# Decoding 64-bit weights without the folding pass, with the range check on a second load, in a linear-attention and expert kernel

## The chip, the cores and the metric

The kernel runs on one core of a Trainium2 chip. The metric is the device time of one execution in microseconds (us), the median over several runs. A profiled execution gives the trace; it covers the span from the first to the last instruction, and its own device time lies a little above the span. The engines are called PE (TensorE: matmuls; PEld is its weight load), DVE (VectorE), ACT (ScalarE), POOL (GpSimd) and SP (SyncE, which here only issues DMAs).

## What is computed

Two stages. The first is a linear attention with a decay for each key element, over 4 batches, 8 heads, 768 steps and heads of 48; the second is a gated expert layer on the 3072 tokens that come out, of width 384 with 1536 inner columns.

```python
# attention: state is 48 x 48 for each batch and head
for t in range(S):
    state = alpha[:, :, t, :, None] * state + einsum('bhd,bhe->bhde', k[:, :, t], v[:, :, t])
    y[:, :, t] = einsum('bhd,bhde->bhe', q[:, :, t], state)
# expert layer: x is y as 3072 x 384
xn = x / sqrt(mean(x * x, axis=-1, keepdims=True) + 1e-06) * rms_g
g, val = xn @ w_gate, xn @ w_val                       # 384 x 1536 each
out = (g * (1 / (1 + exp(-g))) * val) @ w_out          # 1536 x 384
```

q, k, v, alpha and rms_g are fp32. The three weights come as 64-bit floats, and the kernel sees each as one 64-bit integer, that is as two 32-bit words: `lo` (the last 32 bits of the fraction) and `hi` (sign, 11 bits of exponent, 20 of fraction).

## The kernel before

**Precision.** Every operand of a matmul is split in two f16 numbers, a high part (the value cast to f16, mostly by ACT) and a low part (what is left, mostly by DVE), and each product is three matmuls: high by high, high by low, low by high (`SPLIT`).

**Chunks and groups.** The tokens are cut in 24 chunks of 128 (6 for each batch, the batches in turn), and the chunks in seven groups, `GROUPS = [4, 2, 2, 4, 4, 4, 4]`. For a chunk, `attention` does on DVE two scans (L643) with a reciprocal between, the products of q and k with the decays (L661, L666) and the low parts (L673, L691, L700); on ACT the high parts (L477, in the helper `split_hi`, which also sums what it writes into a column of `stat`); on PE the scores (L741, L750), the output y (L821, L831) and the update of the state (L849). The masked scores (L756) are cast by ACT (L808); their low part is taken by DVE (L811) or, for the chunks in `LOW_A`, by a matmul with a negative identity (L792) and ACT (L802). Then come the RMS norm (L873 on ACT, L879 and L893 on DVE, a power on POOL), x in two parts (L897 on ACT, L900 on DVE) and its transpose by DMA into xT (L911, on SP's queue).

**Expert layer.** For a group and each of 12 steps of 128 inner columns, `expert_in` does two halves of nine matmuls (L1029), gate and value, each into one of three `mm` buffers in PSUM; ACT takes the silu of the gate (L1040), DVE multiplies by the value (L1046), ACT casts the high part of h (L477) and DVE takes the low part (L1059). Group 0's first `EARLY = 5` steps are done twice, for two chunks each. After its 12 steps a group's output is summed by `expert_out`: 36 matmuls for each chunk (L1099) into `mm_po`, which is one of the same three `mm` buffers, evacuated by DVE into `ob` (L1113) and stored (L1117). Group 0's four chunks are done as three and one (`SIDE`).

**Weights.** `decode` turns a tile of 128 x 768 64-bit words into f16 high and low parts, for 12 input tiles i0 to i11 (w_gate and w_val, 786 KB by two DMAs, L504) and 6 output tiles o0 to o5 (w_out, one DMA). Two `raw` and two `wu` buffers hold the tiles in work. The steps for one tile are:

- the fold, ACT (L514): |hi| times 2^-111 as an fp32, written to the compact words `u`; it brings the exponent in range, drops the sign, and its accumulated sum goes to `wsum` for a range check
- the tail, DVE (L523): `lo` shifted right by 29
- the sign: for 11 tiles (`SIGN_A`) ACT writes an f16 zero of the right sign into the top half of each `lo` word (L532, an f16 at every 8 bytes); for the others DVE puts it there with the sign bit of `hi` (L526)
- the join, DVE (L537): `u` shifted left by 3, or `lo`, which is the fp32 word
- the high part, ACT (L477, with its sum in `stat`), and the low part, DVE (L545). For the tiles of `LOW_W`, i0 and i6, the join goes to two `y` buffers in PSUM (L556), and the low part is made by a matmul with a negative identity (L566, after PE has claimed the buffers at L550) and ACT (L572).

At the end `verdict` compares the sums in `stat`, `ssq`, `wsum` and `dec` with bounds; if one is outside, a branch runs `general`, a slow version for any input.

**The order of the work.** Nothing above is issued in the order of the code. Each step is an operation with an engine, a cost and the buffers that it uses, and `Plan.order` sorts all of them once, with a due time for each that comes from the tables at the top (`PACE`, `GAP`, `FIRST_DUE`, `AHEAD`, `STRIDE`, `LATE`, `NUDGE`, `HOLD`). The outcome is one fixed queue of instructions for each engine, DMA issues on SP among them; an engine runs its queue strictly in order and waits at the head for what is not done yet.

Of the kernel before, what the change touches and what calls it, by code (L numbers as in the profile page):

```python
# [81 lines left out]
LATE = dict(
    abs=-6.0, al=-47.4, claim=73.0, gd=-9.8, h=-40.7, hl=79.1, join=-68.1, join2=22.9,
    k16=-35.5, kl=33.1, load=7.2, mask=-8.5, neg=-6.2, ob=-61.3, po=138.5, q16=57.8, ql=37.3,
    rec=-14.7, rest=-50.9, sc=-9.9, scan=23.1, sd=12.9, sign=39.5, sl=-13.0, sq=-22.1, ss=-57.2,
    st=0.5, u=-55.5, v16=6.0, vl=-2.7, wh=9.4, wh2=34.9, wl=-23.8, wneg=-1.0, x=-3.2, x16=-27.9,
    xl=-107.4, y=-20.0, zero=-6.0,
)
# [240 lines left out]
def tile_attn_moe(  # L329
# [134 lines left out]
    o_x = o_h + NH  # L464
    o_kk = o_x + len(LOW_W)
# [28 lines left out]
    def decode(src, dst, name, col):  # L494
# [4 lines left out]
        def load():  # L499
# [9 lines left out]
            t["top"] = raw.bitcast(F16).rearrange("p (n four) -> p n four", four=4)[:, :, 1]  # L509
            t["hif"] = raw.bitcast(F32).rearrange("p (n two) -> p n two", two=2)[:, :, 1]  # L510

        def fold():
# [1 line left out]
            nc.scalar.activation(  # L514
                t["u"].bitcast(F32),
                t["hif"],
                AF.Abs,
                scale=W_FOLD,
                accum_out=wsum[:, col - o_w : col - o_w + 1],
            )  # L520

        def tail_bits():
            nc.vector.tensor_scalar(t["lo"], t["lo"], 29, None, op0=ALU.logical_shift_right)  # L523

        def sign():
            nc.vector.scalar_tensor_tensor(  # L526
                t["lo"], t["hi"], -(2**31), t["lo"], op0=ALU.bitwise_and, op1=ALU.bitwise_or
            )

        def sign_zero():  # L530

            nc.scalar.activation(t["top"], t["hif"], AF.Copy, scale=W_NONE)  # L532

        half = [slice(n * (NW // 2), (n + 1) * (NW // 2)) for n in range(2)]

        def join():
            nc.vector.scalar_tensor_tensor(  # L537
                t["u"], t["u"], 3, t["lo"], op0=ALU.logical_shift_left, op1=ALU.bitwise_or
            )
# [4 lines left out]
        def low():
            nc.vector.tensor_tensor(dst[:, 1], t["u"].bitcast(F32), dst[:, 0], op=ALU.subtract)  # L545
# [9 lines left out]
        def join_at(n):  # L555
            nc.vector.scalar_tensor_tensor(  # L556
                t["ps"][n].bitcast(I32)[:, : NW // 2], t["u"][:, half[n]], 3, t["lo"][:, half[n]],
                op0=ALU.logical_shift_left, op1=ALU.bitwise_or,
            )
# [16 lines left out]
        oa = add("ACT", "abs", fold, [o], [raw, wu])  # L576
        ot = add("DVE", "rest", tail_bits, [o], [raw], lock=True)
        if name in SIGN_A:
            os = add("ACT", "zero", sign_zero, [ot], [raw])
# [766 lines left out]
```

## Time and profile before

| | before |
|---|---|
| median of 3 runs | 536.62 us (536.5 to 537.01) |
| the profiled execution | 537.63 us, of which 535.4 are the span |
| granted TensorE clock, mean | 0.997 |
| PE busy | 498.2 us (93%), 4808 matmuls |
| DVE busy | 397.4 us (74%), 743 instructions |
| ACT busy | 269.0 us (50%), 695 instructions |
| POOL busy | 22.5 us (4%) |
| DMA | 50.51 MB, mean 94 GB/s |

The page of the profile has the span in 40 slices of 13.4 us, with the busy share of each engine in tenths. A line for a group of instructions gives the line of the code, the engine, the operation with what it writes and reads, the count, the busy time, the mean of one in ns, and the idle time just before it with what ended most of that. In the table of stretches each engine has its busy time and count, and behind them stand the granted clock, the busy share of the DMA engines and GB/s. In a list of waits stand the sum in us, the count and the longest. In the chain and the timeline stand the start and the length in us.

### The profile page before, as it was taken

What the parts mean: (1) busy time and instruction counts of PE and PEld (TensorE: products, weight loads), DVE (VectorE), ACT (ScalarE), POOL (GpSimd) and SP (SyncE); (2) the same over time, 40 slices, a digit from 0 to 9 for tenths busy, and PEclk for the clock granted to TensorE, in tenths of its full rate; (3) what the DMA queues carried; (4) which work ended last, traced back from release to release, by engine and by line L of the source; (5) the groups of instructions that cost most, each with busy time, mean ns of one, the idle gap of its engine ahead of it and who ended that gap; (6) DMA issues with size and microseconds to landing.
All of it is one profiled execution on the core that took longest, in us unless ns stands there. A gap on an engine that the chain in (4) does not pass through costs nothing.

```text
span 535.4 us, 11809 instructions
## 1 busy us (share of the span) xinstructions
PE 498.2 (93%) x4808; PEld 298.9 (56%) x4808; DVE 397.4 (74%) x743; ACT 269.0 (50%) x695; POOL 22.5 (4%) x55
## 2 busy tenths in 40 slices
PE   1548699899999999999999999999999999999996
PEld 1437464466886887544566544556545555544453
DVE  6998889999999999995799956899767541133331
ACT  3889989854655565433554434645256420133300
POOL 3001000001000100000000000000000000000000
PEclk9999989999999999999999999999999999999999
DMA  8997747553543631951034820412100001000001
GB/s 193 254 256 211 211 150 227 189 151 98 141 99 91 126 86 27 202 117 53 1 84 115 185 75 1 99 36 61 45 16 16 5 13 44 31 0 2 0 16 47
DMA packets 59435, 50.51 MB, mean 94 GB/s; under 512 B 39441, under 2 KB 54929, under 8 KB 59377
## 3 DMA queue, kind: packets, MB, share of 16 engines
q1 hardware_dynamic: 59232, 49.52, 37.1%
q8 instruction: 38, 0.62, 0.5%
q14 instruction: 21, 0.16, 0.1%
q10 hardware_dynamic: 144, 0.20, 0.1%
HBM read 35.68 MB, written 4.72 MB: 75 GB/s over the span
## 4 chain that ended last, share of the span: by engine, by line
PE 79%; DVE 8%; ACT 7%; issue 2%; DMA 2%; SPq 0%; DVEq 0%; ACTq 0%
PE mm L1029 46%; PE mm_po L1099 23%; PE at L741 3%; PE y L831 2%; PE y L821 2%; ACT raw_i L532 2%; PE at L849 1%; ACT wu_i L514 1%; DMA raw_o<-w_out 1%; ACT wg L477 1%; DVE at L756 1%; DMA raw_i<-w_val 1%; DVE dk L643 1%; DVE wu_o L537 1%; DVE raw_o L526 1%
## 5 line engine op out<-in xcount | busy, mean ns | idle before, releaser
L1029 PE MATMUL mm<-xT,wg 128*128 128x512 f16 (+1 forms) x1602 | 290.6, 341 | 6.8 <-ACT sl L1040 3.1
L1029 PEld LDWEIGHTS <-wg 128*128 128x128 f16 x1602 | 155.7, 99 | 130.8 <-issue 6.3
L1099 PE MATMUL mm_po<-wo,h 128*128 128x384 f16 x864 | 146.0, 326 | 1.9 <-DVE h L1046 1.2
L1099 PEld LDWEIGHTS <-h 128*128 128x128 f16 x864 | 82.6, 98 | 56.7 <-issue 3.0
L477 ACT ACTIVATE h<-h 128x512 f16<-128x512 f32 (+1 forms) x89 | 48.9, 549 | 88.6 <-DVE h L1046 88.4
L1046 DVE SCALAR_TENSOR_TENSOR h<-mm,sl 128x512 f32<-128x512 f32 (+1 forms) x89 | 51.7, 584 | 46.8 <-PE mm L1029 46.1
L1040 ACT ACTIVATE sl<-mm 128x512 f32<-128x512 f32 (+1 forms) x89 | 45.6, 514 | 50.9 <-PE mm L1029 50.5
L1059 DVE TENSOR_TENSOR h<-h,h 128x512 f16<-128x512 f32 (+1 forms) x89 | 51.4, 583 | 22.9 <-ACT h L477 22.8
L643 DVE TENSOR_TENSOR_SCAN dk<-att,seed 112x520 f32<-112x520 f32 x48 | 59.3, 1236 | 2.8 <-DMA att<-att 2.3
L889 POOL TENSOR_TENSOR ss<-ss,mhalf 128x1 f32<-128x1 f32 x24 | 16.9, 705 | 419.8 <-DVE ss L879 419.8
L1113 DVE TENSOR_SCALAR ob<-mm_po 128x384 f32<-128x384 f32 x24 | 13.0, 547 | 27.3 <-PE mm_po L1099 26.9
L756 DVE TENSOR_TENSOR at<-at,mask 128x512 f32<-128x512 f32 x48 | 31.0, 689 | 2.7 <-PE at L741 2.6
L808 ACT CAST a<-at 128x512 f16<-128x512 f32 x48 | 27.3, 582 | 10.7 <-DVE at L756 10.4
L831 PE MATMUL y<-v,a 128*128 128x48 f16 x576 | 27.7, 187 | 3.3 <-ACT a L802 3.0
L831 PEld LDWEIGHTS <-a 128*128 128x128 f16 x576 | 23.6, 99 | 5.1 <-ACT a L802 3.3
L811 DVE TENSOR_TENSOR a<-at,a 128x512 f16<-128x512 f32 x38 | 24.6, 681 | 0.1
L477 ACT ACTIVATE k<-kh 112x512 f16<-112x512 f32 x24 | 15.0, 626 | 18.3 <-PE at L741 10.4
L821 PE MATMUL y<-s,q 112*128 112x96 f16 x240 | 22.7, 204 | 0.0
L873 ACT ACTIVATE junk<-y 128x384 bf16<-128x384 f32 x24 | 11.8, 491 | 21.4 <-DVE x L893 12.8
L532 ACT ACTIVATE raw_i<-raw_i 128x768 f16<-128x768 f32 x10 | 19.3, 1925 | 0.0
L750 PE MATMUL at<-qp,kh 48*128 48x128 f32 x64 | 8.5, 438 | 11.5 <-DVE qp L666 10.1
L893 DVE TENSOR_TENSOR x<-y,rg 128x384 f32<-128x384 f32 x24 | 13.2, 550 | 5.9 <-PE y L831 4.3
(106 smaller groups left out, 425.6 us busy)
## 6 DMA issues: line engine op xcount, KB each, us to landing
att<-att SPq DMA_DIRECT2D x22, 675.9 KB, 5.2
v<-vtok SPq DMA_DIRECT2D x24, 192.0 KB, 3.6
raw_i<-w_gate SPq DMA_DIRECT2D x12, 384.0 KB, 4.8
raw_i<-w_val SPq DMA_DIRECT2D x12, 384.0 KB, 5.7
raw_o<-w_out SPq DMA_DIRECT2D x6, 768.0 KB, 4.7
out_dram<-ob SPq DMA_DIRECT2D x23, 192.0 KB, 2.1
att<-att SPq DMA_DIRECT2D x2, 448.0 KB, 7.0
att<-att SPq DMA_DIRECT2D x2, 227.9 KB, 3.1
```

Of the source, the lines that this page charges most:

```text
L477: nc.scalar.activation(dst, src, AF.Copy, scale=scale, accum_out=stat[:rows, col : col + 1])
L532: nc.scalar.activation(t["top"], t["hif"], AF.Copy, scale=W_NONE)
L643: nc.vector.tensor_tensor_scan(out, x, start.rearrange("r g p c -> r (g p c)"), 0.0, op0=ALU.mult, op1=ALU.add)
L756: nc.vector.tensor_tensor(t["sc"][j], t["sc"][j], mask[:, int(not sc16)].to_broadcast([P, NP, C]), op=ALU.mult,)
L808: nc.scalar.copy(a_tile()[:, j, 0], t["sc"][j])
L821: nc.tensor.matmul(yps[:, 2 * p * D : 2 * (p + 1) * D], t["q16"][:, x, p, :], s16_tile()[:, y, p].rearrange("r j e -> r (j e)"), start=m == 0,
L831: nc.tensor.matmul(yps[:, (2 * p + j) * D : (2 * p + j + 1) * D], a_tile()[:, j, x, p, :], t["v16"][:, y, p, j, :], start=first and m == 0 ...
L1029: nc.tensor.matmul(ps[:, :n], wg[:, f, x, j, kk, :], xT[:, y, kk, cs], start=i == 0, stop=i == 3 * NK - 1,)
L1040: nc.scalar.activation(t["sl"][:, :n], t[0][:, :n], AF.Silu, scale=1.0 / (S_X * S_W))
L1046: nc.vector.scalar_tensor_tensor(t["h"][:, :n], t[1][:, :n], S_H / (S_X * S_W), t["sl"][:, :n], op0=ALU.mult, op1=ALU.mult,)
L1059: nc.vector.tensor_tensor(h16_of(g, f)[:, 1, cs], t["h"][:, :n], h16_of(g, f)[:, 0, cs], op=ALU.subtract)
L1099: nc.tensor.matmul(t[i][:, :DM], h16_of(g, f)[:, x, ts], wo[:, f // 2, y, f % 2, :], start=f == 0 and m == 0, stop=f == NF - 1 and m == 2,)
```

## The change

**The word is joined without the fold.** `hi` shifted left by 3 already holds the low bits of the exponent and the fraction; what the fold did to the exponent is done by flipping one bit and by a factor. For the tiles whose sign DVE sets, the tail also sets two constant bits (`FLIP`), and the join combines `hi` << 3 with it by xor. The tiles in `SIGN_H` leave the constant bits out: their words are 2^128 times too large with the opposite sign, and the `scale` of the cast to the high part, of the low part and, in PSUM, of the identity (`plus_w`, in bf16) takes that away again. The factor of the weights, 2^8, moves into the same `scale`.

**Signs go to the compact words.** For the ten tiles in `SIGN_H` DVE writes the shifted tail to the compact words `wu` (L528), and ACT writes its f16 zero with the sign into the top half of those (L533, an f16 at every 4 bytes). i1 and i9 lose ACT's sign pass, i10 gains it. `LOW_W` gains the tile o1.

**The sums for the range check come from a second load.** `inspect` loads each of the 18 raw tiles again, held back to 260 + 9 x n us of the plan, masks the top bits of `hi` (DVE, L630), and sums them (ACT, L634) and the high parts (ACT, through `split_hi`, now L480). `verdict` waits for these and compares `wsum` with an exact value.

**The tables have new numbers**, so the order changes on every engine. The diff, cut to its core (the long tables by one line each):

```diff
-W_FOLD = 2.0**-111
-W_TOP = 2.0**-98
+FLIP = -(2**30)
+W_TOP_BITS, W_TOP_F = 0x78000000, 2.0**-15
...
-SIGN_A = ["i0", "i1", "i2", "i4", "i5", "i6", "i7", "i8", "i9", "i11", "o0"]
-LOW_W = ["i0", "i6"]
+SIGN_H = ["i0", "i2", "i4", "i5", "i6", "i7", "i8", "i10", "i11", "o0"]
+LOW_W = ["i0", "i6", "o1"]
...
-GAP = [0, 15.4, 10.2, -4.5, -15.8, 14.5, 2.8, 70.3]
+GAP = [0, 23.4, 19.6, -10.8, -16.6, 17.6, -4.7, 72.8]
...
-    c8=84.0, i0=17.2, i1=4.6,
+    c1=1.7, c6=57.5, c7=64.0, c8=57.9, c9=56.2,
 )
+CHECK_AT, CHECK_STEP = 260.0, 9.0
...
-    for x, value in ((minus, -1.0), (same, 1.0)):
+    for x, value in ((minus, -1.0), (minus_w, -1.0 / S_W), (plus_w, 2.0**128 / S_W)):
...
-        def fold():
-            t["u"] = buf(wst, [P, NW], I32, "wu", name)
-            nc.scalar.activation(
-                t["u"].bitcast(F32),
-                t["hif"],
-                AF.Abs,
-                scale=W_FOLD,
-                accum_out=wsum[:, col - o_w : col - o_w + 1],
-            )
-
         def tail_bits():
-            nc.vector.tensor_scalar(t["lo"], t["lo"], 29, None, op0=ALU.logical_shift_right)
+            nc.vector.tensor_scalar(
+                t["lo"], t["lo"], 29, FLIP, op0=ALU.logical_shift_right, op1=ALU.bitwise_or
+            )
...
-        def sign_zero():
-
-            nc.scalar.activation(t["top"], t["hif"], AF.Copy, scale=W_NONE)
+        def word():
+            return tile_of(("wu", name), lambda: buf(wst, [P, NW], I32, "wu", name))
+
+        def tail_word():
+            nc.vector.tensor_scalar(word(), t["lo"], 29, None, op0=ALU.logical_shift_right)
+
+        def sign_half():
+
+            top = word().bitcast(F16).rearrange("p (n two) -> p n two", two=2)[:, :, 1]
+            nc.scalar.activation(top, t["hif"], AF.Copy, scale=W_NONE)
+
+        def join_word():
+            nc.vector.scalar_tensor_tensor(
+                word(), t["hi"], 3, word(), op0=ALU.logical_shift_left, op1=ALU.bitwise_xor
+            )
...
+        by_half = name in SIGN_H
+        scale = -S_W * 2.0**-128 if by_half else S_W
+        away = plus_w if by_half else minus_w
...
-                t["u"], t["u"], 3, t["lo"], op0=ALU.logical_shift_left, op1=ALU.bitwise_or
+                word(), t["hi"], 3, t["lo"], op0=ALU.logical_shift_left, op1=ALU.bitwise_xor
...
-            split_hi(dst[:, 0], t["u"].bitcast(F32), col)
+            nc.scalar.activation(dst[:, 0], word().bitcast(F32), AF.Copy, scale=scale)
...
-            nc.vector.tensor_tensor(dst[:, 1], t["u"].bitcast(F32), dst[:, 0], op=ALU.subtract)
+            nc.vector.scalar_tensor_tensor(
+                dst[:, 1], word().bitcast(F32), scale, dst[:, 0], op0=ALU.mult, op1=ALU.subtract
+            )
...
+    def inspect(src, dst, name, col, hold):
...
+        def top_bits():
+            u = buf(wst, [P, NW], I32, "wu", name)
+            t["u"] = u.bitcast(F32)
+            nc.vector.tensor_scalar(u, t["hi"], W_TOP_BITS, None, op0=ALU.bitwise_and)
+
+        def range_sum():
+            c = col - o_w
+            nc.scalar.activation(t["u"], t["u"], AF.Copy, accum_out=wsum[:, c : c + 1])
+
+        def high_sum():
+            split_hi(t["u"], dst[:, 0], col)
...
+    for i in range(NWT):
+        sums_of_w.append(inspect(w_src[i], w_dst[i], f"s{i}", o_w + i, CHECK_AT + CHECK_STEP * i))
...
-        nc.vector.tensor_scalar(iw, wsum, W_TOP, None, op0=ALU.is_le)
+        nc.vector.tensor_scalar(iw, wsum, NW * W_TOP_F, None, op0=ALU.is_equal)
```

What the order becomes is shown at three places. The rows are instructions in the order of an engine's queue: the line, the operation, what is written and read, and the size. The first place is ACT's queue at the first weight tile, `raw_i_161`, from its fold to its high part, before:

```order
L514 ACTIVATE wu_i_264,wsum<-raw_i_161 128x768
L873 ACTIVATE junk,ssq<-y_238 128x384
L808 CAST a_1_269<-at_0_219 128x512
L808 CAST a_1_269<-at_1_220 128x512
L532 ACTIVATE raw_i_161<-raw_i_161 128x768
L897 ACTIVATE x_0_283<-x_0_273,ss_271 128x384
L514 ACTIVATE wu_i_286,wsum<-raw_i_165 128x768
L802 CAST a_1_269<-at_0_219 128x512
L802 CAST a_1_269<-at_1_220 128x512
L532 ACTIVATE raw_i_165<-raw_i_165 128x768
L477 ACTIVATE wg,stat<-wu_i_264 128x768
```

The same place of ACT's queue now, where the first tile, `raw_i_166`, is one that goes through the PSUM buffers `y_i_0_273` and `y_i_1_274`:

```order
L533 ACTIVATE wu_i_277<-raw_i_166 128x768
L856 CAST a_1_286<-at_0_255 128x512
L856 CAST a_1_286<-at_1_256 128x512
L945 ACTIVATE x_0_291<-x_0_268,ss_270 128x384
L574 ACTIVATE wg<-y_i_0_273 128x384
L574 ACTIVATE wg<-y_i_1_274 128x384
L850 CAST a_1_286<-at_0_255 128x512
L585 ACTIVATE wg<-y_i_0_273 128x384
L585 ACTIVATE wg<-y_i_1_274 128x384
L850 CAST a_1_286<-at_1_256 128x512
```

The folds are gone, and the sign pass (L533) is the first thing that ACT does for a tile; no second tile's pass stands between it and the high part.

The second place is DVE's queue at the weight tile i4, from its tail to its join, before (`x` is a chunk's normed tokens, `h` what `expert_in` makes):

```order
L523 TENSOR_SCALAR raw_i_465<-raw_i_465 128x768
L893 TENSOR_TENSOR x_3_639<-y_579,rg 128x384
L1046 SCALAR_TENSOR_TENSOR h_0_1_0_695<-mm_1_0_1_562,sl_1_0_619 128x256
L1059 TENSOR_TENSOR h_0_0_605<-h_0_0_0_554,h_0_0_605 128x256
L1046 SCALAR_TENSOR_TENSOR h_0_2_0_708<-mm_2_0_1_625,sl_2_0_642 128x256
L537 SCALAR_TENSOR_TENSOR wu_i_623<-wu_i_623,raw_i_465 128x768
```

And now, where the row of L691 with `dk` is one of a later chunk's scans:

```order
L528 TENSOR_SCALAR wu_i_634<-raw_i_507 128x768
L1094 SCALAR_TENSOR_TENSOR h_0_0_0_650<-mm_0_0_1_584,sl_0_0_597 128x256
L1094 SCALAR_TENSOR_TENSOR h_0_1_0_653<-mm_1_0_1_622,sl_1_0_632 128x256
L554 SCALAR_TENSOR_TENSOR wg<-wu_i_618,wg 128x768
L691 SCALAR_TENSOR_TENSOR dk_679<-att_241,seed 112x520
L536 SCALAR_TENSOR_TENSOR wu_i_634<-raw_i_507,wu_i_634 128x768
```

Four instructions of other work stand between the tail and the join both times; now they are a low part of another tile and a scan in place of rows of h and x, and the tail's result goes to the compact words.

The third place is SP's queue where the x of group 4 (chunks 12 to 15) is transposed into `xT`, before:

```order
L911 DMA_TRANSPOSE xT_4128<-x_13_4255 128x6x128
L1117 DMA out_dram<-ob_0_4294 128x384
L405 DMA att_4329<-att 112x1545
L1117 DMA out_dram<-ob_1_4426 128x384
L911 DMA_TRANSPOSE xT_4128<-x_14_4444 128x6x128
L677 DMA_TRANSPOSE kT_4557<-k_14_3981 128x8x112
L410 DMA v_4573<-vtok 128x384
L911 DMA_TRANSPOSE xT_4128<-x_15_4570 128x6x128
```

And now, with the second loads of the raw tiles (`raw_s`, L622):

```order
L959 DMA_TRANSPOSE xT_3932<-x_13_4137 128x6x128
L407 DMA att_4255<-att 112x1545
L622 DMA raw_s_4269<-w_gate 128x3x128
L622 DMA raw_s_4269<-w_val 128x3x128
L959 DMA_TRANSPOSE xT_3932<-x_14_4297 128x6x128
L622 DMA raw_s_4381<-w_gate 128x3x128
L622 DMA raw_s_4381<-w_val 128x3x128
L1165 DMA out_dram<-ob_0_4397 128x384
L622 DMA raw_s_4540<-w_gate 128x3x128
L622 DMA raw_s_4540<-w_val 128x3x128
L959 DMA_TRANSPOSE xT_3932<-x_15_4476 128x6x128
```

Three second loads, each of two DMAs, now stand ahead of or between the last two transposes of that group.

More of the change, by code (lines that the diff above doesn't have):

```diff
@@ L6 @@
 from concourse._compat import with_exitstack
+BF16 = mybir.dt.bfloat16
 F16 = mybir.dt.float16
@@ L74 @@
 LOAD_SLOW = (7.4, 160.0)
-PACE = [0.95, 0.882, 0.939, 1.188, 0.85, 0.983, 1.632, 1.156]
-GAP = [0, 15.4, 10.2, -4.5, -15.8, 14.5, 2.8, 70.3]
-FIRST_DUE = [-19.8, -20.6, 17.8, -5.4]
-AHEAD = [-0.8, 26.7, -3.0, 21.8, 24.1, 26.1, 12.2, -35.5]
-STRIDE = [-1.6, 21.2, 19.5, 24.4, 8.7, 7.7, 18.0, 80.4]
-LATE = dict(
[L83 to L87, printed above, removed]
+PACE = [0.967, 0.87, 1.171, 1.159, 0.85, 0.982, 1.625, 0.918]
@@ L455, in tile_attn_moe @@
         nc.gpsimd.memset(rare[rows], 1e6 * (S_X / S_Y[h]) ** 2)
-    junk = const.tile([P, DM], mybir.dt.bfloat16, name="junk")
+    junk = const.tile([P, DM], BF16, name="junk")
     mhalf = const.tile([P, 1], F32, name="mhalf")
@@ L463, in tile_attn_moe @@
     o_h = o_o + NF // 2
[L464 to L465 removed]
+    o_kk = o_h + NH
     o_qq = o_kk + NC
@@ L571, in residue @@
         def residue(n):
-            nc.scalar.copy(dst[:, 1, half[n]], t["ps"][n][:, : NW // 2])
+            nc.scalar.activation(
+                dst[:, 1, half[n]], t["ps"][n][:, : NW // 2], AF.Copy, scale=scale
+            )
         raw, wu = ("raw", name), ("wu", name)
         o = op("SP", 0.9, load, [], [raw], kb=786, late=LATE["load"], hold=HOLD.get(name, 0.0))
[L576 to L579, printed above, removed]
+        if by_half:
+            ot = add("DVE", "rest", tail_word, [o], [raw, wu], lock=True)
+            os = add("ACT", "zeroh", sign_half, [ot], [raw, wu])
         else:
+            ot = add("DVE", "rest", tail_bits, [o], [raw], lock=True)
             os = add("DVE", "sign", sign, [ot], [raw], lock=True)
@@ L591, in decode, with load @@
             return out
-        o = add("DVE", "join", join, [oa, os], [raw, wu], lock=True)
+        o = add("DVE", "join", join_word if by_half else join, [os], [raw, wu], lock=True)
         o = add("ACT", "wh", high, [o], [wu])
         return add("DVE", "wl", low, [o], [wu], lock=True)
+    def inspect(src, dst, name, col, hold):
+        t = {}
+        who[0] = name
+        def load():
+            raw = buf(wst, [P, NW], I64, "raw", name)
+            for i, ap_in in enumerate(src):
+                h = NW // len(src)
+                w = ap_in.shape[-1]
+                nc.sync.dma_start(
+                    raw[:, i * h : (i + 1) * h].rearrange("p (k f) -> p k f", f=w), ap_in
+                )
+            t["hi"] = raw.bitcast(I32).rearrange("p (n two) -> p n two", two=2)[:, :, 1]
+        def top_bits():
[7 more added lines that the diff above has]
+            split_hi(t["u"], dst[:, 0], col)
+        raw, wu = ("raw", name), ("wu", name)
+        o = op("SP", 0.9, load, [], [raw], kb=786, due=hold + 40, hold=hold)
+        o = op("DVE", 0.55, top_bits, [o], [raw, wu], due=hold + 45, lock=True)
+        o = op("ACT", 0.92, range_sum, [o], [wu], due=hold + 50)
+        return op("ACT", 0.92, high_sum, [o], [wu], due=hold + 60)
     states = {}
@@ L1259, in tile_attn_moe @@
     work, pst, pok = ("raw", "work"), ("at", "pst"), ("at", "pok")
-    v = op("POOL", 2.0, lambda: next(it), list(w_ops.values()), [work], due=now - 60)
-    v = op("ACT", 0.5, lambda: next(it), [v] + marks, [work], due=now - 24)
+    v = op("POOL", 2.0, lambda: next(it), list(w_ops.values()) + sums_of_w, [work], due=now - 60)
+    v = op("ACT", 0.5, lambda: next(it), [v] + marks + sums_of_w, [work], due=now - 24)
     v = op("PE", 0.4, lambda: next(it), [v], [work, pst], due=now - 22)
```

78 lines of the change are left out of this document (44 added, 34 removed).

## The prediction

> **What bounds the kernel now.** I read the page first: its first lines and the slices of PE, DVE and ACT.
>
> ```profile
> span 535.4 us, 11809 instructions
> PE 498.2 (93%) x4808; PEld 298.9 (56%) x4808; DVE 397.4 (74%) x743; ACT 269.0 (50%) x695; POOL 22.5 (4%) x55
> PE   1548699899999999999999999999999999999996
> DVE  6998889999999999995799956899767541133331
> ACT  3889989854655565433554434645256420133300
> ```
>
> PE is full from the tenth slice on; before that DVE and ACT are. Then the busy time by stretch (columns: stretch, its length, then PE, PEld, DVE, ACT, POOL busy with counts).
>
> ```profile
> 20.00:100.00 80.00, 63.35 (x559) 39.80 (x559) 70.65 (x124) 74.26 (x170) 3.67 (x4) 0.98 0.79 207
> 100.00:130.00 30.00, 27.70 (x390) 17.06 (x390) 29.55 (x51) 17.54 (x44) 2.42 (x7) 1.00 0.48 138
> sum 130.00, PE 97.38 PEld 61.72 DVE 115.24 ACT 100.75 POOL 11.03; mean PE 24.35 PEld 15.43 DVE 28.81 ACT 25.19 POOL 2.76
> 130.00:260.00 130.00, 130.00 (x1456) 89.94 (x1455) 118.54 (x242) 67.29 (x205) 4.43 (x6) 1.00 0.45 102
> 260.00:450.00 190.00, 190.00 (x1924) 106.07 (x1923) 140.24 (x261) 84.78 (x219) 7.06 (x12) 1.00 0.23 55
> ```
>
> In the first 130 us PE is idle 130 - 97.4 = 32.6 us, and from 130 to 450 not at all. So the time is PE's work plus what PE loses ahead of about 130 us. Where that ends the timeline of PE shows, and the chain its pace and its end:
>
> ```profile
> 129.02 6.01 PE L1099 MATMUL mm_po<-wo,h 128*128 128x384 f16 x36 [0.64 <-DVE ob L1113]
> 460.11 46.62 PE mm L1029 x216
> 517.36 4.50 PE mm_po L1099 x27
> 530.89 0.56 DVE ob L1113
> ```
>
> At 129.02 PE waits for the last time, for DVE's first evacuation of an output block (ob of group 0); it then works without a gap to the last evacuation at 530.89. Hence the one quantity to forecast is when DVE reaches that ob, beside the PE work that is done by then. DVE's queue up to it is nearly full (100.2 of the 110 us from 20 to 130), so it matters what DVE waited for there:
>
> ```profile
> DVE wu_i L537 <- ACT raw_i L532: 5.3, 7, 1.3
> DVE h L1059 <- ACT h L477: 0.7, 1, 0.7
> DVE wu_o L537 <- ACT raw_o L532: 0.6, 1, 0.6
> DVE wg L545 <- ACT wg L477: 0.5, 2, 0.3
> DVE ss L879 <- ACT junk L873: 0.4, 2, 0.2
> DVE y_i L556 <- ACT raw_i L532: 0.3, 1, 0.3
> ```
>
> ACT's sign pass (L532) is what DVE waits for: 5.3 + 0.6 + 0.3 = 6.2 us. ACT is 74.3 of 80 us busy there, so it comes late.
>
> **The change part by part.** The rows that price the decoding of a weight tile:
>
> ```profile
> L514 ACT ACTIVATE wu_i<-raw_i 128x768 f32<-128x768 f32 x12 | 11.1, 924 | 0.5 <-DMA raw_i<-w_val 0.3
> L514 ACT ACTIVATION_READ_ACCUMULATOR wu_i<-raw_i 128x1 f32 x12 | 2.4, 199 | 0.0
> L532 ACT ACTIVATE raw_i<-raw_i 128x768 f16<-128x768 f32 x10 | 19.3, 1925 | 0.0
> L477 ACT ACTIVATE wg<-wu_i 128x768 f16<-128x768 f32 x10 | 8.6, 855 | 0.1
> L477 ACT ACTIVATION_READ_ACCUMULATOR wg<-wu_i 128x1 f32 x10 | 2.0, 195 | 0.0
> L477 ACT ACTIVATE wg<-y_i 128x384 f16<-128x384 f32 x4 | 1.9, 483 | 0.0
> L523 DVE TENSOR_SCALAR raw_i<-raw_i 128x768 int32<-128x768 int32 x12 | 6.6, 552 | 0.0
> L526 DVE SCALAR_TENSOR_TENSOR raw_i<-raw_i 128x768 int32<-128x768 int32 x2 | 1.9, 949 | 0.0
> L537 DVE SCALAR_TENSOR_TENSOR wu_i<-wu_i,raw_i 128x768 int32<-128x768 int32 x10 | 9.6, 959 | 5.6 <-ACT raw_i L532 5.3
> L545 DVE TENSOR_TENSOR wg<-wu_i,wg 128x768 f16<-128x768 f32 x10 | 9.5, 951 | 0.5 <-ACT wg L477 0.5
> L556 DVE SCALAR_TENSOR_TENSOR y_i<-wu_i,raw_i 128x384 int32<-128x384 int32 x4 | 2.1, 561 | 0.3 <-ACT raw_i L532 0.3
> ```
>
> *ACT.* Gone are 18 folds with their sums, 18 x (0.92 + 0.20) = 20.2 us, and the sums of the high parts, 16 x 0.195 + 4 x 0.2 = 3.9. One weight tile more (o1) goes through PSUM: four passes of 0.48 for one of 0.86, +1.1. Ten sign passes take the place of eleven. Each now writes every second f16 of the compact words, not every fourth of the raw ones. The trace has no such form; its bounds are 0.86 (the contiguous 768-column pass) and 1.93 (the old one). I take 1.93, the nearest row, since it differs in the distance alone: -1.9. Together ACT sheds 20.2 + 3.9 - 1.1 + 1.9 = 24.9 us of the 100.75 ahead of 130.
>
> [...]
>
> *DVE.* Counted in the built order with the rows' means, 191 instructions of 125.5 us stand ahead of that ob before, and 190 of 124.4 now: one sign +0.95, one join less -0.96, two half joins +1.12, one residue less -0.95, and the rest attention rows, -1.3. That is -1.1 us. The residue now also scales; by the other two-operation rows it costs the same.
>
> *The waits for the sign pass.* Between a tile's first DVE pass and its join, DVE's queue held 1.5 to 2.3 us of other work for eight of the eleven tiles of before; now it holds 2.1 to 3.0 for all ten. Against 1.93 and hops of under 0.1 (88.96 + 1.83 to 90.81 in the chain below), and with ACT no longer full, I leave 0.8 of the 6.2: -5.4. If ACT still comes late, up to 2.5 stay. ACT's other delays (0.7 + 0.5 + 0.4 = 1.6): -1.0, between 0 and -1.6.
>
> *The head.* The second part of the first attention tile is loaded second, no longer third:
>
> ```profile
> DVE kh L661 <- DMA att<-att: 1.2, 1, 1.2
> ```
>
> That wait goes, but the k and v residues that now follow wait for ACT: -0.4, between 0 and -1.2.
>
> *What comes late next.* The two raw buffers: a tile's load can only start when the join two tiles earlier is done. In the chain:
>
> ```profile
> 82.40 4.61 DMA raw_i<-w_val
> 88.96 1.83 ACT raw_i L532
> 90.81 0.97 DVE wu_i L537
> 91.80 5.78 DMA raw_o<-w_out
> ```
>
> Load 5.8, first pass 0.55, sign 0.95 and join 0.96 are 8.3 us for the five output tiles that DVE signs, 4.1 a tile, and DVE's queue takes about 4 there; I add +1.0, between 0 and 2. The low part of chunk 4's x stands behind the ob as well:
>
> ```profile
> 128.44 0.99 DVE L1113 TENSOR_SCALAR ob<-mm_po 128x384 f32<-128x384 f32 x2
> 129.76 0.61 DVE L900 SCALAR_TENSOR_TENSOR x<-x,ss,x 128x384 f16<-128x384 f32 x1
> ```
>
> It came 1.3 us after the ob; now 3.3 us of rows lie between, and its transposed DMA (2.8 to 4 us, below) must land within the 6.0 us of PE's 36 matmuls: +0.7, between 0 and 1.5. PE has four matmuls of 384 columns more, at the chain's 4.50 / 27 = 0.167: +0.7; the conversion of a bf16 identity beside f16 data is not in the trace, and I cost it at nothing, since only four matmuls have it.
>
> *The late reload.* 18 tiles x 786 KB = 14.2 MB from about 260 us on, by SP's queue; each with a DVE pass of 0.55 and two ACT passes of 1.05 (0.86 with its 0.195): 18 x 2.1 = 37.8 us of ACT beside 84.8 of 190, 9.9 of DVE beside 140.2, and 75 GB/s beside 55 where the head moves 207. All of it lies beside PE's work, and a late silu has the room of two matmul groups (2 x 9 x 46.62 / 216 = 3.9 us), as there are three mm buffers. I cost it at nothing; without that cover see the second rival.
>
> **Sum**: -1.1 - 5.4 - 1.0 - 0.4 + 1.0 + 0.7 + 0.7 = -5.5 us against the profiled execution's own 537.63 (535.4 and 2.2 around it): 532.1. The runs' median is 536.62, 1.0 lower, so the forecast for a median is **531.1**. With every term at its good end, -1.1 - 6.2 - 1.6 - 1.2 + 0.7 = -9.4, and 1 more for a sign pass of 0.86: 526.2. At the bad end -1.1 - 3.7 - 0 - 0 + 2 + 1.5 + 0.7 = -0.6: 536.0.
>
> **The rivals.**
>
> *DVE is the bound until 270.* From that ob to the gate of group 3's last step DVE had 265 instructions of 147.8 us; it now has 291 of 164.2: attention work that was done early is put off. Some 14 us of it are real, as neighbours overlap. Room for it are the 11.5 us that DVE idled from 130 to 260, some 2 until 270, and 4 us by which PE's queue between the same points is longer in the built order: about 18. It fits by 4 us; if new waits take 6 to 8, then 2 to 4 come back: 533 to 535. Against it: 4 us are more than the waits that DVE shows there.
>
> *The reloads hold up the transposes* (slower). In SP's queue the loads stand ahead of the x transposes of groups 4 and 5.
>
> ```profile
> raw_i<-w_val SPq DMA_DIRECT2D x12, 384.0 KB, 5.7
> DMA to landing us min/median/max: 2.8/4.0/9.3
> ```
>
> A load took 5.7 us to land, and x transposes among such loads (20 to 140 us) up to 9.3, where 2.8 is the least. [...] If the last x of groups 4 and 5 lands 6 us late without slack, PE stalls 12: 536.6 - 5.5 + 12 = 543. It decides against the change from 5.5 us on. Against it: PE waited for no x after 130, and DMA is 23% busy from 260 to 450.
>
> *Nothing gained*: the head is held by something that both have, DMA or DVE's own chain, and the sign pass's wait comes back elsewhere; 536 to 537.
>
> **How the numbers follow.** The sum 0.63; DVE the bound 0.15; nothing gained 0.06; reloads hold up 0.16. Two runs of this kernel differ by up to 0.1%, so about 0.2% (1.1 us) is what a measurement can tell. Faster 0.63 + 0.15 = 0.78, same 0.06, slower 0.16. The range runs from the good end, 526, through the second case and the bad end to 537; it leaves out the reloads' case and little else.
>
> **What would show it.** Right: PE's last wait ahead of 260 us comes 5 to 6 us earlier than 129; DVE's waits for the sign pass fall below 1.5 us; ACT is under 60 of the 80 us from 20 to 100; no wait of PE from 260 to 450. Wrong: PE idle after that ob, for DVE (first rival) or for xT (second); or a sign pass above 2 us with DVE waiting for it as before.

## The result and the profile after

The changed kernel takes 527.7 us (median of 4 runs, 527.44 to 529.15) where the kernel before takes 536.82 (4 runs, 536.5 to 538.08). The ratio is 0.9831, with a 95% interval of 0.9807 to 0.9855: 9.1 us less. The profiled execution took 527.79 us, against 537.63 before. Its page begins so:

```profile
span 526.1 us, 11850 instructions
PE 498.3 (95%) x4812; PEld 298.6 (57%) x4812; DVE 404.6 (77%) x762; ACT 272.9 (52%) x713; POOL 22.0 (4%) x57
PE   1769999899999999999999999999999999999996
DVE  7999999999999999999965999996566830233330
ACT  3768767454655662556444567856557630233300
```

PE does the same 498 us of work in a span that is 9.3 us shorter, so what went is idle time of PE. DVE is now full from the second slice to the twentieth, ACT in none. The table of stretches (length, then PE, PEld, DVE, ACT, POOL busy with counts, granted clock, DMA share, GB/s) shows where:

```profile
20.00:100.00 80.00, 70.55 (x651) 44.23 (x650) 77.84 (x134) 57.27 (x138) 1.89 (x3) 1.00 0.82 220
100.00:125.00 25.00, 24.37 (x331) 15.34 (x329) 24.63 (x46) 11.47 (x26) 1.10 (x2) 1.00 0.36 104
125.00:260.00 135.00, 135.00 (x1615) 93.42 (x1604) 131.30 (x267) 74.03 (x224) 5.55 (x8) 1.00 0.45 102
260.00:450.00 190.00, 190.00 (x1810) 105.02 (x1807) 131.91 (x248) 104.84 (x267) 6.80 (x15) 1.00 0.47 126
```

From 20 to 100 us ACT is busy 57.3 us, not 74.3, and DVE 77.8, not 70.7; PE gains 7.2 us there. From 125 to 450 PE has no gap; the kernel before had none from 130 on. DVE's waits in the first 125 us, all that the list has (line waited for, us in total, times, longest):

```profile
DVE dk L691 <- DMA att<-att: 2.2, 1, 2.2
DVE wu_i L528 <- DMA raw_i<-w_val: 1.1, 1, 1.1
DVE seed L422 <- PEq L1384: 1.0, 1, 1.0
DVE h L1094 <- PE mm L1077: 0.5, 1, 0.5
DVE k L721 <- ACT k L480: 0.3, 1, 0.3
```

No wait for the sign pass is in the list any more, where there were 6.2 us. DVE reaches group 0's first output block 11 us earlier. First the sums up to that block before (128.44 us), then now (117.39):

```profile
sum 128.44, PE 96.41 PEld 61.13 DVE 113.68 ACT 99.44 POOL 11.03; mean PE 96.41 PEld 61.13 DVE 113.68 ACT 99.44 POOL 11.03
```

```profile
117.39 1.01 DVE L1161 TENSOR_SCALAR ob<-mm_po 128x384 f32<-128x384 f32 x2
sum 117.39, PE 94.76 PEld 60.15 DVE 111.09 ACT 74.01 POOL 9.13; mean PE 94.76 PEld 60.15 DVE 111.09 ACT 74.01 POOL 9.13
```

Of the 11.05 us, 2.6 are DVE's busy time (113.68 to 111.09) and 8.5 its idle time (128.44 - 113.68 = 14.76 to 117.39 - 111.09 = 6.30). PE's last wait in the whole changed kernel comes 9 us ahead of the block, and is for a cast by ACT:

```profile
108.22 0.86 PE L840 MATMUL at<-a,minus 128*128 128x512 f16 x2 [0.29 <-ACT a L856]
```

The rows that price a weight tile now:

```profile
L533 ACT ACTIVATE wu_i<-raw_i 128x768 f16<-128x768 f32 x9 | 9.6, 1066 | 3.3 <-DVE wu_i L528 3.1
L551 ACT ACTIVATE wg<-wu_i 128x768 f16<-128x768 f32 x10 | 8.4, 845 | 3.4 <-DVE wu_i L536 2.6 <-DVE wu_i L546 0.7
L554 DVE SCALAR_TENSOR_TENSOR wg<-wu_i,wg 128x768 f16<-128x768 f32 x10 | 9.5, 950 | 0.1
L630 DVE TENSOR_SCALAR wu_s<-raw_s 128x768 int32<-128x768 int32 x18 | 9.9, 556 | 1.3 <-DMA raw_s<-w_val 1.0 <-issue 0.2
L634 ACT ACTIVATE wu_s<-wu_s 128x768 f32<-128x768 f32 x18 | 15.1, 838 | 10.5 <-DVE wu_s L630 10.5
```

The sign pass with f16 at every 4 bytes takes 1.07 us, not 1.93. ACT now waits for DVE ahead of it (3.1 us), where before DVE waited behind it.

### The profile page after: what moved, and what is told of

Read it like the earlier page. It is cut to its first block, busy times and chain, and to the rows that moved or that the text cites. A ratio compares the mean times of both kernels' runs of the same rounds, so it can differ in the third digit from the quotient of the medians.

```text
span 526.1 us, 11850 instructions
## 1 busy us (share of the span) xinstructions
PE 498.3 (95%) x4812; PEld 298.6 (57%) x4812; DVE 404.6 (77%) x762; ACT 272.9 (52%) x713; POOL 22.0 (4%) x57
## 4 chain that ended last, share of the span: by engine, by line
PE 82%; DVE 11%; ACT 1%; issue 1%; DMA 1%; DVEq 0%; ACTq 0%
PE mm L1077 48%; PE mm_po L1147 25%; PE at L789 3%; PE y L879 3%; PE y L869 2%; PE at L897 1%; DVE h L1107 1%; DVE dk L691 1%; DVE h L1094 1%; DVE wg L554 1%; DVE wu_i L536 1%; DVE raw_o L520 1%; DVE wu_o L546 1%; DMA xT<-x 1%; DVE wu_i L528 0%
## 5 line engine op out<-in xcount | busy, mean ns | idle before, releaser
L1077 PEld LDWEIGHTS <-wg 128*128 128x128 f16 x1602 | 153.8, 98 | 122.7 <-issue 2.5
L480 ACT ACTIVATE h<-h 128x512 f16<-128x512 f32 (+1 forms) x89 | 48.5, 545 | 63.1 <-DVE h L1094 62.8
L1107 DVE TENSOR_TENSOR h<-h,h 128x512 f16<-128x512 f32 (+1 forms) x89 | 51.3, 583 | 16.5 <-ACT h L480 16.5
L691 DVE TENSOR_TENSOR_SCAN dk<-att,seed 112x520 f32<-112x520 f32 x48 | 59.5, 1240 | 2.6 <-DMA att<-att 2.2
L921 ACT ACTIVATE junk<-y 128x384 bf16<-128x384 f32 x24 | 11.8, 490 | 21.0 <-DVE x L941 11.7
L634 ACT ACTIVATE wu_s<-wu_s 128x768 f32<-128x768 f32 x18 | 15.1, 838 | 10.5 <-DVE wu_s L630 10.5
L480 ACT ACTIVATE k<-kh 112x512 f16<-112x512 f32 x24 | 15.0, 625 | 8.0 <-DVE kh L709 4.2
```

What stands on the lines that cost most here:

```text
L480: nc.scalar.activation(dst, src, AF.Copy, scale=scale, accum_out=stat[:rows, col : col + 1])
L691: nc.vector.tensor_tensor_scan(out, x, start.rearrange("r g p c -> r (g p c)"), 0.0, op0=ALU.mult, op1=ALU.add)
L1077: nc.tensor.matmul(ps[:, :n], wg[:, f, x, j, kk, :], xT[:, y, kk, cs], start=i == 0, stop=i == 3 * NK - 1,)
L1107: nc.vector.tensor_tensor(h16_of(g, f)[:, 1, cs], t["h"][:, :n], h16_of(g, f)[:, 0, cs], op=ALU.subtract)
```

## The experiments

Each kernel was timed in five rounds against the kernel before. The ratios are to that; the difference in us is the ratio's, at 536.8 us. An interval of 0.0013 to 0.0027 each way is 0.7 to 1.4 us, so differences of about one microsecond between two kernels are not clear of the scatter.

**1. The old order without the fold.** Every engine's queue is that of the kernel before, less the folds and the sums of fold and high parts; the diff at its core:

```diff
-            nc.scalar.activation(t["u"].bitcast(F32), t["hif"], AF.Abs, scale=W_FOLD, accum_out=...)
...
-                t["u"], t["u"], 3, t["lo"], op0=ALU.logical_shift_left, op1=ALU.bitwise_or
+                t["u"], t["hi"], 3, t["lo"], op0=ALU.logical_shift_left, op1=ALU.bitwise_xor
```

> The kernel before with its old order on every engine, the fold left out and the word joined as in the change; the sums for the range check of the weights are left out too, and the sign still goes to every 8 bytes. ACT sheds some 24 us, DVE nothing. Theory A (ACT's lateness cost the head its time): DVE's waits for the sign pass fall from 6.2 us to 1 or 2, and the time falls by 4 to 6, to 531 to 533. Rival B (the new order brought the gain): less than 2 us, 535 to 537. Rival C (the shorter sign pass brought a good part): with the pass still at 1.93 us half of the waits stay, 533 to 535.

Measured: 531.72 us, ratio 0.9898 (0.9880 to 0.9915), 5.5 us less. The waits for the sign pass (the first line, and 0.2 for an output tile) fall from 6.2 to 3.3, and DVE comes to the block at 122.96:

```profile
DVE wu_i L543 <- ACT raw_i L536: 3.1, 7, 0.7
sum 122.96, PE 94.12 PEld 60.12 DVE 113.37 ACT 82.89 POOL 11.55; mean PE 94.12 PEld 60.12 DVE 113.37 ACT 82.89 POOL 11.55
```

Theory A holds by its time but not by its waits (3.3 us, not 1 or 2), and B falls: the old order gives more than half of the gain. By the waits C is right, as half of them stayed; by the time (533 to 535) it is not.

**2. The old order, with the signs in the compact words.** As 1, with the tail and the sign written to `wu`:

```diff
-                nc.vector.tensor_scalar(t["lo"], t["lo"], 29, None, op0=ALU.logical_shift_right)
+                nc.vector.tensor_scalar(word(), t["lo"], 29, None, op0=ALU.logical_shift_right)
...
-            nc.scalar.activation(t["top"], t["hif"], AF.Copy, scale=W_NONE)
+            top = word().bitcast(F16).rearrange("p (n two) -> p n two", two=2)[:, :, 1]
+            nc.scalar.activation(top, t["hif"], AF.Copy, scale=W_NONE)
```

> As no_fold, same order on every engine, and the sign written to the compact words at every 4 bytes, as in the change (1.07 us a pass, not 1.93). Theory A: 0.5 to 1 us below no_fold, 530 to 532, since few waits are left. Rival C: 2 to 4 us below no_fold. Rival B: no change from no_fold, both at 535 to 537.

Measured: 528.88 us, ratio 0.9848 (0.9833 to 0.9864), 8.2 us less, and 2.7 below experiment 1. That is C's range, and not A's 0.5 to 1. No wait of DVE for the sign pass is listed any more. With the old numbers in the tables all but 0.9 us of the gain is there. The block comes at 117.80:

```profile
sum 117.80, PE 92.36 PEld 59.57 DVE 112.13 ACT 75.06 POOL 11.52; mean PE 92.36 PEld 59.57 DVE 112.13 ACT 75.06 POOL 11.52
```

**3. The changed kernel without the second load.** The operations stay in the plan and do nothing, so that the order of the others is unchanged; two memsets stand in for the sums.

```diff
-        o = op("SP", 0.9, load, [], [raw], kb=786, due=hold + 40, hold=hold)
-        o = op("DVE", 0.55, top_bits, [o], [raw, wu], due=hold + 45, lock=True)
+        o = op("SP", 0.9, lambda: None, [], [raw], kb=786, due=hold + 40, hold=hold)
+        o = op("DVE", 0.55, lambda: None, [o], [raw, wu], due=hold + 45, lock=True)
```

> The changed kernel in its own order without the second loads of the weights, their DVE pass and their two ACT passes (the range check of the weights is left out). Theory A: the late reload is hidden beside PE's work, so the time is that of the changed kernel within 0.2%, 527 to 528.5. Rival D (the reload costs something by its DMA or by ACT): 1 us or more below, under 526.7.

Measured: 528.77 us, ratio 0.9831 (0.9816 to 0.9847), the same ratio as the changed kernel's. 14.2 MB, 7.6 us of DVE's busy time (404.6 and 397.0) and 29.4 of ACT's (272.9 and 243.5) cost nothing that can be measured. Behind the block the profiled executions take the same time with the second loads and without, 410.4 and 410.3 us (529.32 - 119.01). Theory A holds by the ratio.

**4. The changed kernel with signs at every 8 bytes**, the reverse of the edit of experiment 2, in the new order.

> The changed kernel in its own order, the sign pass at every 8 bytes of the raw words, as before (1.93 us a pass, not 1.07; ACT +8.6 us). Theory A, with the forecast's own size for this term: up to 1 us slower, 528 to 529. Rival C (the shorter pass is what the forecast lacked): 3 to 4 us slower, 531 to 532. No change at all would say that ACT has slack throughout.

Measured: 530.19 us, ratio 0.9860 (0.9842 to 0.9879): 1.6 us slower than the changed kernel, between A and C and nearer to A; the intervals overlap. (Against experiment 3, timed in the same rounds, it is 1.4 by the medians.) DVE's wait for the sign pass comes back with 0.5 us:

```profile
DVE wu_i L535 <- ACT raw_i L532: 0.5, 2, 0.3
```

That is near the 0.8 us that the forecast left for this price of the pass, and the block comes 0.5 us later than in experiment 3 (119.55 and 119.01), whose profile has the same drop of the clock ahead of it (last section). The new order covers the pass better: at 1.93 us a pass DVE waits 0.5 us for it here and 3.3 in the old order. In the time the two orders (1.6 us for the pass here, 2.7 there) are not clearly apart.

**5. DVE's tail done twice** on the ten tiles with an ACT sign, order unchanged:

```diff
             nc.vector.tensor_scalar(word(), t["lo"], 29, None, op0=ALU.logical_shift_right)
+            nc.vector.tensor_scalar(word(), t["lo"], 29, None, op0=ALU.logical_shift_right)
```

> The changed kernel, DVE's first pass of the ten tiles with an ACT sign (0.555 us each) done twice, +5.6 us of DVE ahead of group 0's first output block, the order otherwise the same. Theory A (DVE's queue is what the head's time follows, now that it hardly waits): 4 to 5.5 us slower than the changed kernel, 532 to 534. Rival E (PE waits for ACT's casts and for x instead): under 2 us slower.

Measured: 531.87 us, ratio 0.9899 (0.9881 to 0.9917), 3.7 us slower than the changed kernel. The sums up to the block:

```profile
sum 121.28, PE 94.83 PEld 59.83 DVE 116.43 ACT 74.53 POOL 9.36; mean PE 94.83 PEld 59.83 DVE 116.43 ACT 74.53 POOL 9.36
```

DVE's busy time grew by 5.3 us, its idle time shrank by 1.5 (6.30 to 4.85), and the block and the kernel both came 3.9 us later (profiled executions, 527.79 and 531.72). That is a little less than Theory A's 4, and well above Rival E's 2, which falls.

**6. The changed kernel without DVE's signs**: `sign` does nothing.

> The changed kernel without DVE's sign pass on the eight tiles that have one (the signs of these weights are left out), -7.6 us of DVE ahead of group 0's first output block, the order otherwise the same. Theory A: 4 to 7 us faster than the changed kernel, 521 to 524, and less than the full 7.6 as other waits come up. Rival E: under 2 us faster, 526 or more.

Measured: 524.85 us, ratio 0.9771 (0.9749 to 0.9793), 3.2 us faster than the changed kernel.

```profile
DVE wu_i L526 <- DMA raw_i<-w_val: 1.4, 2, 1.3
DVE x L939 <- ACT junk L919: 1.1, 1, 1.1
DVE raw_o L515 <- DMA raw_o<-w_out: 0.9, 1, 0.9
sum 114.51, PE 93.56 PEld 60.02 DVE 104.07 ACT 74.06 POOL 9.16; mean PE 93.56 PEld 60.02 DVE 104.07 ACT 74.06 POOL 9.16
```

DVE's busy time fell by 7.0 us, its idle time grew by 4.1, and the block came 2.9 earlier. Both theories missed: less than A's 4 and more than E's 2. DVE's queue is the longest chain of the head, but after some 3 us of gain it waits for others (raw loads, ACT, PE).

**7. The kernel before, ordered by the new tables**: only the numbers from `PACE` to `HOLD` are exchanged.

> The kernel before, with its fold and all its sums, ordered by the planner with the change's tables (the order that comes out is not the one of the changed kernel, since the steps differ). Theory A (the work saved is the gain): 535 to 539. Rival B (the new numbers bring the gain): 533 or less.

Measured: 551.76 us, ratio 1.0268 (1.0247 to 1.0288), 14 us slower. The new numbers bring nothing by themselves; set for other steps they do harm, which neither theory expected. The block comes 0.6 us earlier than before (127.81), so the whole loss lies behind it, and the stretch there shows where:

```profile
125.00:260.00 135.00, 127.93 (x1593) 92.44 (x1592) 120.90 (x249) 68.06 (x209) 6.30 (x9) 0.96 0.39 99
141.94 0.21 PE L742 MATMUL at<-q,k 48*128 48x128 f16 x1 [1.59 <-ACT q L478]
144.73 1.46 PE L742 MATMUL at<-q,k 48*128 48x128 f16 x23 [2.57 <-DVE a L812]
148.02 2.10 PE L1030 MATMUL mm<-xT,wg 128*128 128x256 f16 x9 [1.83 <-DMA xT<-x]
```

PE is idle 7 us there, for attention work of the next groups, and for an x, that the tables put too late. Much of the rest is slower work: the granted clock of the stretch is 0.96, where the kernel before has 1.00, and among these waits 23 matmuls of the scores take 1.46 us (the row at 144.73), where 24 took 0.84 at 139.51. PE is busy 505.9 us in all, not 498.2.

**8. The kernel before without its sums**: `accum_out` is taken from the fold and the high parts.

> The kernel before in its old order with the fold, and without the accumulated sums of fold and high parts (the range check of the weights is left out): ACT sheds 18 x 0.2 + 3.9 = 7.5 us, a third of what no_fold takes away. Theory A with a gain in proportion: 1.5 to 2 us faster than before, 534.8 to 535.3. Rival F (the fold's own place ahead of the sign pass in ACT's queue is what delays it, the sums are not): under 0.7 us, 536 or more.

Measured: 535.57 us, ratio 0.9970 (0.9957 to 0.9983), 1.6 us less. ACT's busy time falls by 3.3 us (269.0 to 265.7), not by the 7.5 of the rows, as a sum's read-out overlaps with what follows: the one at 23.35 us in the profile before lasts 0.20 us, and the next row starts at 23.44. In experiment 1 ACT's busy time falls by 16.5 (to 252.5), not by the 24 of the rows, for 5.5 us of time. For each microsecond that ACT sheds, the sums thus bring no less than fold and sums together (1.6 for 3.3, 5.5 for 16.5). Theory A's time came, and Rival F falls.

**9. The second load early.** `CHECK_AT, CHECK_STEP = 125.0, 5.0`.

> The changed kernel with the second loads held back to 125 + 5 x n us of the plan, not 260 + 9 x n; up to about 120 us the order is the same, behind it the planner sorts anew. 9.9 us of DVE and 37.8 of ACT move into the stretch where DVE is already busy 131 of 135 us. Theory G (DVE is close to being the bound until 270, the forecast's first rival): 3 us slower than the changed kernel or more, 531 and up. Theory A (room remains there, since PE's queue is long): under 1 us, 527 to 529.

Measured: 529.66 us, ratio 0.9853 (0.9827 to 0.9879): 1.2 us slower than the changed kernel, within the uncertainty of both. Of the 18 tiles 12 fall ahead of 260 us, from 199 us on. With 18 us more of ACT in the stretch PE has one gap, of 0.52 us:

```profile
125.00:260.00 135.00, 134.48 (x1617) 92.66 (x1615) 131.97 (x272) 92.40 (x270) 6.70 (x8) 1.00 0.66 169
211.82 7.95 PE L1077 MATMUL mm<-xT,wg 128*128 128x512 f16 x36 [0.52 <-DMA xT<-x]
```

DVE's busy time there is hardly changed (131.97, from 131.30): the planner let other DVE work slide behind 260, where there is room. Theory G falls. By the runs A is not settled to a microsecond; the profiled executions are for it, as this one takes 529.56 us and that of experiment 3, without second loads and with the same clock of 0.98 from 20 to 100 us (last section), 529.32.

**10. ACT's sign pass done twice**, order unchanged (the line in `sign_half` repeated).

> The changed kernel with ACT's sign pass done twice on each of its ten tiles (+10.7 us of ACT, 2.14 us from the tail to the join's release), the order the same. Theory A (ACT has room now; only the tiles with little cover wait): 2 to 3 us slower, 530 to 531. Rival H (DVE's join waits for the whole of it): 6 us slower or more, 534 and up.

Measured: 531.06 us, ratio 0.9884 (0.9867 to 0.9902), 2.8 us slower than the changed kernel, as A has it: 10.7 us of ACT cost a quarter of themselves.

**11 and 12. More signs to ACT**, nothing left out: `SIGN_H` with o1 to o5, and `SIGN_H` with i3. Both let the planner sort anew.

> The changed kernel with ACT doing the sign of all six output tiles (five more), nothing left out; the planner sorts anew from the output tiles on. DVE sheds 5 x 0.95 = 4.8 us, ACT takes 5 x 1.07 = 5.4. Theory A (the time follows DVE's first output block): 2 to 4 us faster than the changed kernel, 524 to 526. Rival I (with two raw buffers the loads of the output tiles set the pace, and the sign's place on another engine changes nothing there): within 1 us of the changed kernel, or slower.

> The changed kernel with ACT doing the sign of i3 as well, nothing left out; DVE sheds 0.95 us, ACT takes 1.07, and the order moves a little. Theory A, by the slope of the run without DVE's signs (2.9 us of the first output block for 7.6 us of DVE): 0.4 us faster. Rival I: no change, or slower by the wait for the sign.

Measured: 534.91 us, ratio 0.9956 (0.9940 to 0.9971), and 532.22 us, ratio 0.9905 (0.9878 to 0.9932): 6.7 and 4.0 us slower than the changed kernel. Theory A fails in both. In the run with i3, DVE, SP and PE around the block:

```profile
117.03 1.00 DVE L1161 TENSOR_SCALAR ob<-mm_po 128x384 f32<-128x384 f32 x2
124.34 0.59 DVE L948 SCALAR_TENSOR_TENSOR x<-x,ss,x 128x384 f16<-128x384 f32 x1
124.96 1.21 SPq L959 DMA_TRANSPOSE xT<-x  x1
128.68 2.08 PE L1077 MATMUL mm<-xT,wg 128*128 128x256 f16 x9 [3.15 <-DMA xT<-x]
```

The block comes no later than in the changed kernel. But the new sorting puts the low part of the next group's x three and a half microseconds further behind, and PE waits 3.15 us for it, after 0.80 for the block; behind these waits the matmuls are slower, nine in 2.08 us where the changed kernel does 90 in 10.00, and the granted clock from 125 to 260 us is 0.99, not 1.00. In the changed kernel the same rows stand so:

```profile
120.82 0.59 DVE L948 SCALAR_TENSOR_TENSOR x<-x,ss,x 128x384 f16<-128x384 f32 x1
121.44 1.21 SPq L959 DMA_TRANSPOSE xT<-x  x1
125.01 10.00 PE L1077 MATMUL mm<-xT,wg 128*128 128x256 f16 x90
```

There the transpose is issued 3.6 us ahead of the matmuls, and PE does not wait. In the run with o1 to o5 PE waits 2.46 us for the same x, and 2.13 us ahead of the block for the low part of an output tile; its block comes 2.9 us later (120.27): the tables have numbers for certain steps, and no longer fit when one moves. Rival I named the outcome, but not the cause: in that run no wait of DVE for a raw load is listed. What the signs on ACT would bring in an order made for them stays open, and no version here that leaves nothing out beats the changed kernel.

## Why the prediction was right, and by how much it fell short

It forecast 531.1 us, a gain of 5.5; measured were 527.7 and 9.1. The direction and the mechanism hold, the size was too small.

**The quantity to forecast.** The claim was that the time is set by when DVE reaches group 0's first output block. Block and time of the profiled executions:

| kernel | block at | time | time less block |
|---|---|---|---|
| before | 128.44 | 537.63 | 409.2 |
| 8, without sums | 126.12 | 535.32 | 409.2 |
| 1, without fold | 122.96 | 531.95 | 409.0 |
| 2, and signs at 4 bytes | 117.80 | 526.88 | 409.1 |
| the changed kernel | 117.39 | 527.79 | 410.4 |
| 3, without second load | 119.01 | 529.32 | 410.3 |
| 4, signs at 8 bytes | 119.55 | 530.08 | 410.5 |
| 5, tail twice | 121.28 | 531.72 | 410.4 |
| 6, without DVE's signs | 114.51 | 524.95 | 410.4 |
| 10, sign twice | 119.17 | 529.83 | 410.7 |
| 9, second load early | 118.64 | 529.56 | 410.9 |
| 12, i3 by ACT | 117.03 | 532.60 | 415.6 |
| 11, o1 to o5 by ACT | 120.27 | 534.71 | 414.4 |
| 7, old steps, new tables | 127.81 | 552.21 | 424.4 |

In the first four rows, the old order, the last column is constant to 0.2 us while the block moves by 10.6; in the next six, the new order, to 0.4 while it moves by 6.8. This is the claim, shown. The last four rows, which the planner sorted anew, show its limit: there PE waits behind the block. (The profiled execution of experiment 2 was the shortest of its four.)

Of the signs named for a right forecast three came: no wait of DVE for the sign pass is listed, ACT is busy 57.3 of the 80 us from 20 to 100, and PE has no wait from 260 to 450. The fourth failed: PE's last wait ahead of 260 us is no longer for the block, and comes 21 us earlier, not 5 or 6 (108.22, 0.29 us, for a cast by ACT). This wait moves with the block (112.11 in experiment 5, 3.9 us later, as the block), so the same chain seems to hold both.

**The terms of the sum**, in the profiled executions:

| term | forecast | measured |
|---|---|---|
| DVE's queue up to the block | -1.1 | -2.6 |
| waits for the sign pass | -5.4 | -6.2 |
| waits for ACT otherwise | -1.0 | -1.6 |
| the head's attention load, with the new wait for k | -0.4 | -0.9 |
| waits for raw tiles | +1.0 | +0.9 |
| other idle time of DVE | 0 | -0.7 |
| PE's work and waits behind the block | +1.4 | +1.2 |
| sum | -5.5 | -9.9 |

The step that fell short is the pricing of DVE's way to the block by the waits alone. The queue was counted rightly (125.5 us of durations before, 124.4 now), but its neighbours overlap, and they overlap more where DVE does not stop between them: 125.5 - 113.68 = 11.8 us before, 124.4 - 111.09 = 13.3 now. The old order shows it with one queue: with the waits shorter but still there (experiment 1) DVE's busy time up to the block is 113.37 us, with none for the sign pass (experiment 2) 112.13, of which 0.3 are shorter rows. A wait thus cost its idle time and the lost overlap as well, 1.5 us of the 3.6 by which the forecast fell short of the runs. The small idle gaps went with the named ones.

The sign pass was priced by the row nearest to it, 1.93, and the lower bound was 0.86; it measured 1.07. What that is worth is 1.6 us in the new order (experiment 4), so with the price of 1.07 the sum would still have been about 2 us short (9.1 - 5.5 - 1.6). The 1 us that the good end adds for a pass of 0.86 is the author's estimate, and no run shows it: with f16 at 8 bytes' distance the pass took more than twice the time of a contiguous one (1.93 us against 0.85), at 4 bytes' distance 1.07, and between these two lie 1.6 us of time in the new order and 2.7 in the old.

The raw tiles: the size was right by luck, since the place was wrong. The wait is for the load of an input tile, the eighth in DVE's queue: DVE idles 1.07 us ahead of that tile's first pass (L528), until 60.52 us. The load was issued at 54.0 us, when the join two tiles earlier was done (53.04 + 0.95), as the forecast has it; but for the output tiles that DVE signs no wait is listed.

Behind the block, 1.4 forecast and 1.2 measured agree by luck too. The low part of the next x: its 0.7 us did not come, by a margin of 0.9 us. The rows above show the transpose issued 3.6 us before it is needed, and it took 2.7 us to land. Experiments 11 and 12 show what it costs when the margin is gone. The four matmuls more, the other 0.7, stand ahead of the block, where PE is idle 22.6 us anyway. The 1.2 us are another thing: PE has 403.6 us of work left at the block (498.3 - 94.76), not 401.8 (498.2 - 96.41), as the new order puts more of it there, and is spared the 0.64 of wait for the block. The work left is 401.8 in every kernel of the table's first four rows and 403.6 in the next six.

**The order.** From experiment 2 to 3, which differ in the tables and in the tiles of `SIGN_H` and `LOW_W`, it is worth 0.9 us (0.9848 and 0.9831, with intervals of 0.0016 each way: not clearly above nothing). The gain as a whole, each part with about a microsecond of scatter and taken in this sequence: sums 1.6, fold 3.9, the pass at 4 bytes 2.7, order and tiles 0.9, the second load 0.

**The rivals.** DVE as the bound until 270: PE has no gap there, and even 18 us more of ACT and two thirds of the second loads in that stretch cost no more than a microsecond or so (experiment 9). The reloads holding up the transposes: experiment 3 shows no cost. From 255 to 450 us the transposes landed so, first before and then in the changed kernel (least, median, most):

```profile
DMA to landing us min/median/max: 2.7/2.8/3.8
```

```profile
DMA to landing us min/median/max: 2.7/2.8/4.5
```

The worst came 0.7 us later; the 6 us of the rival are nowhere. Nothing gained: fell with experiment 1.

## What to carry to other kernels

When one engine works without a gap from some event on, find that event and price each edit by how far it moves it; here time less event held to 0.4 us within each of two orders, over ten kernels. Relief of a half-busy engine (ACT, 50%) was worth what the full one waited for it, and a little more, because a wait also broke the overlap of the instructions around it (DVE's overlap up to the block is 11.8 us with the waits for the sign pass, 13.3 without). Numbers that set an order belong to the steps that they were set for: taken alone they cost 14 us, and one moved step cost 4, in a wait far from the step. A wait of PE behind the event cost its length (3.15 us in experiment 12) and, here, the slower matmuls that followed it (0.23 us each, where the changed kernel's took 0.11).

## What the runs showed of the hardware

- Two sign passes of ACT over the same input: 1927 ns with an f16 at every 8 bytes of the raw words (experiment 1), 1066 with one at every 4 of the compact words (the changed kernel). A contiguous f16 pass of the same size took 845 (the changed kernel, L551).
- In some executions the granted clock fell in the stretch from 50 to 60 us. Experiment 3's profile has it (0.83), the changed kernel's has not (1.00), with the same instructions up to there:

```profile
50.00:60.00 10.00, 7.59 (x54) 5.80 (x53) 8.46 (x18) 6.04 (x17) 0.00 (x0) 0.83 0.83 218
```

```profile
50.00:60.00 10.00, 8.53 (x77) 7.21 (x77) 9.45 (x21) 7.99 (x23) 0.00 (x0) 1.00 0.70 208
```

PE issues 54 matmuls in that time instead of 77, and the block came at 119.01 instead of 117.39. The same 108 matmuls took 15.54 us and 14.00, and PE had waited longer ahead of them, for a transpose of x, where the clock then fell:

```profile
54.72 15.54 PE L1080 MATMUL mm<-xT,wg 128*128 128x256 f16 x108 [2.41 <-DMA xT<-x]
```

```profile
53.88 14.00 PE L1077 MATMUL mm<-xT,wg 128*128 128x256 f16 x108 [1.47 <-DMA xT<-x]
```

The profiles of experiments 4 and 11 have the same drop (0.83), behind waits of 2.18 and 1.9 us; those of 5 and 6 have none, behind 1.47 and 1.74. From 20 to 100 us as a whole the clock of experiment 3 is 0.98; so is that of experiment 9, behind a wait of 2.5 us, and those of 10 and 12 are 1.00, behind 1.5 and 2.2. So the length of the wait does not decide alone, and what does was not tried. The 1.6 us are about the spread of the runs of the changed kernel, 527.44 to 529.15. The kernel before has a drop too (0.89 from 60 to 70 us, behind a wait of 2.45), and experiments 1 and 2 have none there (1.00). It hardly explains the gain: one run of the kernel before had a mean clock of 1.0 and took 536.86 us, where its median in those rounds was 537.63.
